# A sixteen-row head load ahead of a streaming attention kernel, with two moved steps in its start

## The chip, the core and the metric

The kernel runs on 1 core of one Trainium2 chip. The metric is the device time of one execution in microseconds (us); lower is better. Before and after are compared on the same chip.

## The reference

One decoding step of attention with grouped queries: 32 query heads of 128 numbers, 8 heads of keys and values, 65536 positions each, all in bf16. Four query heads share one key head.

```python
B, Hq, Hkv, Sq, Sk, D = 1, 32, 8, 1, 65536, 128
def reference(q, k, v):
    rep = Hq // Hkv
    k = jnp.repeat(k, rep, axis=1)
    v = jnp.repeat(v, rep, axis=1)
    scores = jnp.einsum("bhqd,bhkd->bhqk", q, k) * D ** -0.5
    p = _softmax(scores, axis=-1)
    return jnp.einsum("bhqk,bhkd->bhqd", p, v)
```

Keys and values are read once: 8 x 65536 x 128 x 2 bytes, twice, which is 268.4 MB.

## The kernel before, in words

**Tiles.** A unit is 16384 positions of one key head: 128 partitions, on each of which lie T = 128 positions of D = 128 numbers, so 32 KB for each partition. There are 4 units for each key head. Two units make a pair; the 16 pairs (NP) are the laps. One pair of keys or of values is 128 rows of 64 KB, 8 MB.

**One lap.** TensorE transposes the keys of a unit in groups of 8 tiles (`pe_transposes`, L131) into four PSUM buffers `trb`; VectorE copies three groups out of four (L197) and ScalarE the fourth (L194) into `ktb`; TensorE multiplies them with the four queries of the head in `qcur` (`pe_scores`, L140). VectorE takes the maximum of the scores (L228), GpSimd reduces it over the partitions (L390), ScalarE computes the exponentials into `pts` (L346), and TensorE multiplies with the values (`pe_values`, L158). A running maximum and sum rescale what was there before.

**Buffers and loads.** SyncE issues all loads of keys and values in order, on one queue. `kbuf` takes 64 KB for each partition, a whole pair of keys; in laps 1 to 12 the second half is copied from there to `bbuf`, by GpSimd and ScalarE (L204, L355), so that `kbuf` comes free early. `vbuf` takes a pair of values. In lap 0 the keys come as four loads of 2 MB, 128 rows of 16 KB each (`K_PIECES`, L404): two into `kbuf` and two into `bbuf`. Then follow two value loads of 128 rows of 32 KB (L434). The next key load (L416) waits until TensorE is through with `kbuf` (`kfree`) and the copies are done (`cfree`); the next value load (L437) waits for `vfree`, which VectorE gives after TensorE's last product of the pair (L293, L306). In the last lap the values come in small pieces, so that TensorE can follow.

**The start.** VectorE builds the identity `ident` that the transposes need, and signals it through `t_id` (L323). ScalarE issues the load of the 32 queries, 8 KB (L371), then waits for `t_id` and runs a small exponential (L373), which brings its table load ahead of it, then copies the identity to float32 (L374). TensorE waits for the queries (`q_sem`) and the identity, transposes the queries (L180), and goes into the laps; its first step there is to wait for the first key piece (`kp[0][0]`). GpSimd clears `lw` and runs one all-reduce on it (L381, L382), whose result is not used, and then waits for the first copies. `own` is a helper that lets an instruction signal a semaphore, waits for that, and takes the signal back:

```python
def own(e, ins, s):
    ins.then_inc(s, 1)
    take(e, s)
```

**The end.** When the last values are multiplied, VectorE scales the last four rows (L303), TensorE transposes them (L185), VectorE copies them out (L336), and SyncE stores them (L448). The other rows are stored before.

Of the kernel before, what the change touches and what calls it, by code (L numbers as in the profile page):

```python
# [10 lines left out]
P = 128  # L11
# [10 lines left out]

K_PIECES = ((64, 64), (64, 64))
V_PIECES = ((128,), (44, 56, 20, 8))

# [11 lines left out]
def starts(sizes):  # L39
    return [sum(sizes[:i]) for i in range(len(sizes))]  # L40


def take(e, sem, n=1):

    e.wait_ge(sem, n)
    e.sem_inc(sem, -n)  # L46


def bass_standalone__gqa_softmax__decode_kernel(nc, q, k, v, out):
# [8 lines left out]
    kf, vf, qf, of = k[0], v[0], q[0, :, 0, :], out[0, :, 0, :]  # L58
# [4 lines left out]
    def sb(name, shape, dt):  # L63
        return S(nc.sbuf_tensor(name, shape, dt))

    def sem(name):
        return S(nc.semaphore(name))

    kbuf = sb("kbuf", [P, 2 * T * D], DT.bfloat16)
# [4 lines left out]
    qsb = sb("qsb", [HR, D], DT.bfloat16)  # L74
# [16 lines left out]
    la = sb("la", [P, R], DT.float32)  # L91
    lw = sb("lw", [P, R], DT.float32)
# [12 lines left out]
    kp = [[sem(f"kp{i}_{p}") for p in range(len(K_PIECES[i]))] for i in range(2)]  # L105
    vp = [[sem(f"vp{i}_{p}") for p in range(len(V_PIECES[i]))] for i in range(2)]
    kfree, cfree, bfree = sem("kfree"), sem("cfree"), sem("bfree")
# [2 lines left out]
    trd, tra, evd, eva = sem("trd"), sem("tra"), sem("evd"), sem("eva")  # L110
    qkd, qrdy, pvd = sem("qkd"), sem("qrdy"), sem("pvd")
    cm, cma, ng, exd, sx, lrd, lra = (sem(n) for n in ("cm", "cma", "ng", "exd", "sx", "lrd", "lra"))
    acr, l_sem = sem("acr"), sem("l_sem")
    xd, xa, xg = sem("xd"), sem("xa"), sem("xg")
    q_sem, o_sem, s_x, t_if, t_id, t_o, t_f, t_row = (
        sem(n) for n in ("q_sem", "o_sem", "s_x", "t_if", "t_id", "t_o", "t_f", "t_row"))
# [4 lines that stand above are left out]
# [24 lines left out]
    def pe_values(pe, n, lap):  # L145
        vv = vbuf[:, n * T * D:(n + 1) * T * D].rearrange("p (t d) -> p t d", d=D)
        for t in range(T):
            if n and t == V_PIECES[1][0]:
                with pe.If(lap == NP - 1):
                    take(pe, acr)  # L150
                    pe.matmul(pvb[n][:, 0:R], lhsT=identf[:, :], rhs=acc[:, :], start=False, stop=False)
            if t == 0:
                take(pe, vp[n][0], 16)
                take(pe, exd)
            piece = vp[n][starts(V_PIECES[n]).index(t)] if t and t in starts(V_PIECES[n]) else None
            if piece:
# [7 lines left out]
    def pe_pair(pe, lap):  # L164
        pend = []
        for n in range(2):
            for j in range(G):
                pe_transposes(pe, n, j)
                pend.append((n, j))
                if len(pend) > LAG:  # L170
                    pe_scores(pe, *pend.pop(0))
        while pend:
            pe_scores(pe, *pend.pop(0))
        for n in range(2):
            pe_values(pe, n, lap)

    def tensor_engine(pe):
        pe.wait_ge(q_sem, 16)
        pe.wait_ge(t_id, 1)
        pe.transpose(qps[:, 0:HR], qsb[:, :], ident[0:HR, 0:HR]).then_inc(s_x, 1)  # L180
        pe.wait_ge(t_if, 1)
        with pe.Fori(0, NP) as lap:
            pe_pair(pe, lap)
        pe.wait_ge(t_f, H)
        pe.transpose(trb[0][0:R, 0:P], oT[:, HR - R:HR], ident[:, :]).then_inc(s_x, 1)  # L185
# [13 lines left out]
    def copy_unit(e, lap, second, copies, op, done, x):  # L199

        def copies_now():
            for c in copies:
                off = T * D + c * CB * D
                ins = op(bbuf[:, c * CB * D:(c + 1) * CB * D], kbuf[:, off:off + CB * D])  # L204
                if c != copies[-1]:
                    ins.then_inc(done, 1)
            own(e, ins, x)
            e.sem_inc(done, 1)

        lo, hi = ((w - second + 1) // 2 for w in WHOLE)  # L210
        with e.If(lap < hi):
            if lo:
                with e.If(lap >= lo):
                    copies_now()
                with e.Else():
                    e.sem_inc(done, len(copies))
            else:
                copies_now()
        with e.Else():
            e.sem_inc(done, len(copies))  # L220
# [131 lines left out]
    def act_pair(e, second, lap):  # L352

        def copy(o, i):
            return e.activation(o, i, AF.Copy)  # L355

        for j in (3, 7, 11, 15):
            evict(e, 0, j)
            if j in ACT_COPIES:
                copy_unit(e, lap, second, ACT_COPIES[j], copy, cpa, xa)  # L360
                if j == max(ACT_COPIES):
                    e.sem_inc(cfree, 1)
        for j in (3, 7):
            evict(e, 1, j)
        exps(e, 0, not second)
        for j in (11, 15):
            evict(e, 1, j)
        exps(e, 1, False)

    def scalar_engine(e):  # L370
        e.dma_start(qsb[:, :], qf).then_inc(q_sem, 16)  # L371
        e.wait_ge(t_id, 1)
        e.activation(dscr[:, 0:1], ident[:, 0:1], AF.Exp, scale=1.0)  # L373
        e.activation(identf[:, :], ident[:, :], AF.Copy).then_inc(t_if, 1)  # L374
        with e.Fori(0, H) as lap:
            act_pair(e, False, lap)
            act_pair(e, True, lap)


    def gpsimd_engine(e):  # L380
        own(e, e.memset(lw[:, :], 0.0), xg)  # L381
        own(e, e.partition_all_reduce(la[:, :], lw[:, :], P, bass.bass_isa.ReduceOp.add), xg)  # L382
        with e.Fori(0, H) as lap:
            for u in range(HU):
                if u % 2 == 0:
                    take(e, pgo)
                    copy_unit(e, lap, u // 2, POOL_COPIES, e.tensor_copy, cpg, xg)
                    e.sem_inc(cfree, 1)
                take(e, cm)
                e.partition_all_reduce(cmaxa[:, :], cmax[:, :], P, bass.bass_isa.ReduceOp.max).then_inc(cma, 1)  # L390
            take(e, lrd)
            e.partition_all_reduce(la[:, :], lp[:, :], P, bass.bass_isa.ReduceOp.add).then_inc(lra, 1)  # L392


    def sync_engine(e):
        W = T * D

        def src(x, p):
            h, c = p // 2, p % 2
            return x[h, c * 2 * P * T:(c + 1) * 2 * P * T, :].rearrange("(p t) d -> p (t d)", p=P)  # L400

        def pieces(to, s, sizes, sems):
            for a, w, sm in zip(starts(sizes), sizes, sems):
                e.dma_start(to[:, a * D:(a + w) * D], s[:, a * D:(a + w) * D]).then_inc(sm, 16)  # L404

        def tokens(sems):
            for sm in sems:
                e.sem_inc(sm, 16)

        for p in range(NP):  # L410
            ks, vs = src(kf, p), src(vf, p)
            if p:
                e.wait_ge(kfree, p)
                e.wait_ge(cfree, 2 * p)
            if WHOLE[0] <= p < WHOLE[1]:
                e.dma_start(kbuf[:, :], ks).then_inc(kp[0][0], 16)  # L416
                tokens(kp[0][1:])
            else:
                for n in range(2):
                    if n and p:  # L420
                        e.wait_ge(bfree, p)
                    to, s = bbuf if n else kbuf, ks[:, n * W:(n + 1) * W]
                    if p in (0, NP - 1):
                        pieces(to, s, K_PIECES[n], kp[n])
                    else:
                        e.dma_start(to[:, 0:W], s).then_inc(kp[n][0], 16)
                        tokens(kp[n][1:])
            if p:
                e.wait_ge(vfree, p)
            if WHOLE[0] <= p < WHOLE[1]:  # L430
                tokens(kp[1])
            if p in (0, NP - 2):
                for n in range(2):
                    e.dma_start(vbuf[:, n * W:(n + 1) * W], vs[:, n * W:(n + 1) * W]).then_inc(vp[n][0], 16)  # L434
                tokens(vp[1][1:])
            elif p < NP - 1:
                e.dma_start(vbuf[:, :], vs).then_inc(vp[0][0], 16)  # L437
                tokens(vp[1])
            else:
                for n in range(2):  # L440
                    pieces(vbuf[:, n * W:(n + 1) * W], vs[:, n * W:(n + 1) * W], V_PIECES[n], vp[n])
        e.wait_ge(t_o, H)
        for b, rows in enumerate(OUT_ROWS):
            for r, n in zip(starts(rows), rows):
                e.dma_start(of[r:r + n, b * Q:(b + 1) * Q],
                            orow[b * Q + r:b * Q + r + n, :]).then_inc(o_sem, 16)
        e.wait_ge(t_row, 1)
        e.dma_start(of[HR - R:HR, :], lrow[:, :]).then_inc(l_sem, 16)  # L448

    with nc.Block() as block:  # L450
        block.tensor(tensor_engine)
        block.vector(vector_engine)
        block.scalar(scalar_engine)
        block.gpsimd(gpsimd_engine)
        block.sync(sync_engine)
# [30 lines left out]
```

## Time and profile before

| | |
|---|---|
| time, median of 3 runs | 629.42 us (629.23 to 629.5) |
| time of the profiled execution | 629.39 us |
| its span, first to last instruction | 627.7 us |
| TensorE, VectorE, ScalarE, GpSimd busy | 78%, 50%, 36%, 24% of the span |
| queue q1 (SyncE's loads and stores) | 268.45 MB, 99.2% of 16 DMA engines |
| mean granted TensorE clock | 0.779 |

How to read it: a line such as L404 is a line of the kernel above. A row of the timeline gives the start and the length in us, the engine, the line, the operation, the output and the input tile. SPq, ACTq and so on are the sequencers of the engines; a load's row on them is its issue alone. In a table of stages, a row gives the stage, its length, the busy time and number of instructions of TensorE (matmuls, then weight loads), VectorE, ScalarE and GpSimd, and then the granted clock, the busy share of the 16 DMA engines and their rate in GB/s. Shares can be a little over 1.00 in short stages.

### The profile page before, as it was taken

The page shows a single profiled execution, that of the slowest core. Times are in us where ns is not written, and L with a number is a line of the kernel's source. Part 1 is how long each engine was busy: PE and PEld are TensorE (multiplying, and loading weights), DVE is VectorE, ACT ScalarE, POOL GpSimd, SP SyncE. Part 2 cuts the span into 40 slices and gives each one's busy share as a digit, 9 for nine tenths or more (in the row PEclk, how much of TensorE's full clock was granted, in tenths as well). Part 3 has the DMA queues.
Part 4 walks back from the last instruction along what each step waited for, and adds up shares of the span by engine and source line. Part 5 has one row for each costly group of instructions (what it writes and reads, how often), then busy time and mean ns, then how long its engine had stood idle before and what let it go on. Part 6 is the DMA issues. An engine that isn't in the chain of part 4 may idle for free. (4 is left out here: it accounts for less than half of the span.)

```text
span 627.7 us, 28345 instructions
## 1 busy us (share of the span) xinstructions
PE 490.6 (78%) x12292; PEld 482.2 (77%) x12292; DVE 315.4 (50%) x698; ACT 227.4 (36%) x435; POOL 148.8 (24%) x118
## 2 busy tenths in 40 slices
PE   4673995949959598695986949779596899789896
PEld 4663995949959598695976949779596899789796
DVE  4540653717537174371744617356183565638282
ACT  2230542515425154341534406244062442414141
POOL 0000703307042070520605115060250700000000
PEclk9865876968869598695987959678596787859596
DMA  8999999999999999999999999999999999999997
GB/s 366 433 455 424 434 430 439 422 447 418 451 418 451 409 455 413 455 413 452 413 455 413 455 413 451 418 451 413 443 426 439 430 418 451 418 432 434 417 437 301
DMA packets 6914, 268.59 MB, mean 428 GB/s; under 512 B 1016, under 2 KB 1016, under 8 KB 1272
## 3 DMA queue, kind: packets, MB, share of 16 engines
q1 hardware_dynamic: 6856, 268.45, 99.2%
q8 instruction: 6, 0.10, 0.1%
q14 instruction: 4, 0.03, 0.0%
q10 hardware_dynamic: 48, 0.01, 0.0%
HBM read 268.44 MB, written 0.01 MB: 428 GB/s over the span
## 5 line engine op out<-in xcount | busy, mean ns | idle before, releaser
L197 DVE COPY ktb<-trb 128x1024 bf16<-128x1024 bf16 x384 | 254.5, 690 | 171.6 <-DVEq L46 170.4
L194 ACT ACTIVATE ktb<-trb 128x1024 bf16<-128x1024 bf16 x128 | 131.0, 1023 | 346.3 <-ACTq L46 346.3
L131 PE MATMUL trb<-ident,kbuf 128*128 128x128 bf16 x2048 | 177.6, 245 | 86.9 <-PEq L46 86.9
L131 PEld LDWEIGHTS trb<-ident,kbuf 128*128 128x128 bf16 x2048 | 144.1, 111 | 87.8 <-issue 87.8
L140 PE MATMUL qkb<-qcur,ktb 128*128 128x4 bf16 x4096 | 176.7, 165 | 15.1 <-PEq L46 10.7
L140 PEld LDWEIGHTS qkb<-qcur,ktb 128*128 128x128 bf16 x4096 | 157.4, 97 | 23.2 <-issue 21.5
L204 POOL COPY bbuf<-kbuf 128x2048 bf16<-128x2048 bf16 x72 | 132.8, 1893 | 153.3 <-POOLq L46 153.3
L131 PE MATMUL trb<-ident,bbuf 128*128 128x128 bf16 x2048 | 159.4, 221 | 3.9 <-issue 3.9
L158 PE MATMUL pvb<-pts,vbuf 128*128 128x4 bf16 x4096 | 112.9, 166 | 23.9 <-PEq L46 14.3
L158 PEld LDWEIGHTS pvb<-pts,vbuf 128*128 128x128 bf16 x4096 | 111.0, 102 | 25.4 <-issue 23.3
L131 PEld LDWEIGHTS trb<-ident,bbuf 128*128 128x128 bf16 x2048 | 119.3, 98 | 1.5 <-issue 1.5
L390 POOL PARTITION_ALL_REDUCE cmaxa<-cmax x32 | 11.9, 370 | 281.6 <-POOLq L46 281.6
L346 ACT ACTIVATE pts<-qkb,negm 128x128 bf16<-128x128 f32 x128 | 50.6, 545 | 0.0
L355 ACT ACTIVATE bbuf<-kbuf 128x2048 bf16<-128x2048 bf16 x24 | 45.7, 1902 | 0.0
L346 ACT ACTIVATION_READ_ACCUMULATOR pts<-qkb,negm 128x1 f32 x128 | 35.4, 277 | 0.0
L228 DVE TENSOR_REDUCE cmax<-qkb 128x4 f32<-128x512 f32 x32 | 21.9, 686 | 17.8 <-DVEq L46 17.8
L256 DVE TENSOR_TENSOR acc<-acc,pvb 128x4 f32<-128x4 f32 x16 | 2.5, 158 | 37.7 <-PE pvb L158 37.7
L342 ACT ACTIVATE alpha<-dm 128x4 f32<-128x4 f32 x24 | 4.9, 203 | 43.4 <-ACTq L46 43.4
L392 POOL PARTITION_ALL_REDUCE la<-lp x8 | 3.4, 429 | 36.9 <-POOLq L46 36.9
L238 DVE TENSOR_TENSOR m<-m,cmaxa 128x4 f32<-128x4 f32 x24 | 3.9, 163 | 11.7 <-DVEq L46 11.5
L247 DVE TENSOR_TENSOR acc<-acc,alpha 128x4 f32<-128x4 f32 x24 | 3.9, 162 | 11.6 <-DVEq L46 11.6
L254 DVE COPY acc<-pvb 128x4 f32<-128x4 f32 x8 | 1.3, 162 | 15.5 <-PE pvb L158 15.5
(41 smaller groups left out, 39.0 us busy)
## 6 DMA issues: line engine op xcount, KB each, us to landing
vbuf<-in_v_dram SPq DMA_DIRECT2D x5, 4096.0 KB, 31.1
kbuf<-in_k_dram SPq DMA_DIRECT2D x4, 2048.0 KB, 16.9
bbuf<-in_k_dram SPq DMA_DIRECT2D x4, 2048.0 KB, 21.7
kbuf<-in_k_dram SPq DMA_DIRECT2D x2, 4096.0 KB, 20.1
bbuf<-in_k_dram SPq DMA_DIRECT2D x2, 4096.0 KB, 19.8
vbuf<-in_v_dram SPq DMA_DIRECT2D x1, 1792.0 KB, 32.2
vbuf<-in_v_dram SPq DMA_DIRECT2D x1, 1408.0 KB, 28.4
vbuf<-in_v_dram SPq DMA_DIRECT2D x1, 640.0 KB, 33.3
```

Source lines behind the costliest of these rows:

```text
L131: ins = pe.transpose(trb[j % NTB][:, i * P:(i + 1) * P], kv[:, t, :], ident[:, :])
L140: ins = pe.matmul(qkb[n][:, t * R:(t + 1) * R], lhsT=ktb[:, off:off + P], rhs=qcur[:, :], start=True, stop=True)
L158: ins = pe.matmul(pvb[n][:, 0:R], lhsT=vv[:, t, :], rhs=pts[n][:, t * R:(t + 1) * R], start=t == 0, stop=t == T - 1)
L194: e.activation(dst, trb[j % NTB][:, :], AF.Copy).then_inc(eva, 1)
L197: e.tensor_copy(dst, trb[j % NTB][:, :]).then_inc(evd, 1)
L204: ins = op(bbuf[:, c * CB * D:(c + 1) * CB * D], kbuf[:, off:off + CB * D])
L228: e.tensor_reduce(cmax[:, :], qkb[n][:, :].rearrange("p (t g) -> p g t", g=R), AX.X, ALU.max).then_inc(cm, 1)
L238: own(e, e.tensor_tensor(mn[:, :], mo[:, :], cmaxa[:, :], ALU.max), xd)
L342: e.activation(alpha[:, :], dm[:, :], AF.Exp, scale=scale)
L346: ins = e.activation(pv[:, g, :], sv[:, g, :], AF.Exp, bias=negm[:, g:g + 1], scale=scale, accum_out=rsum[:, g:g + 1])
L355: return e.activation(o, i, AF.Copy)
L390: e.partition_all_reduce(cmaxa[:, :], cmax[:, :], P, bass.bass_isa.ReduceOp.max).then_inc(cma, 1)
```

## The change

Three edits, all ahead of the first lap or in its first loads.

1. SyncE issues a new first load: rows 0 to 15 of the first unit, 32 KB for each, 512 KB in all, with a semaphore of its own (`h_sem`). The two loads that followed for `kbuf`, 128 rows of 16 KB each, become 112 rows of 16 KB each. TensorE waits for `h_sem` ahead of the laps. The bytes are the same, in one load more.
2. ScalarE issues the load of the queries after the small exponential, and so after its table load and after the wait for the identity.
3. GpSimd waits for its memset on a semaphore of its own and does not take the signal back; the wait behind its all-reduce is gone.

```diff
+HEAD = 16
 ...
         pe.wait_ge(t_if, 1)
+        pe.wait_ge(h_sem, 16)
         with pe.Fori(0, NP) as lap:
 ...
     def scalar_engine(e):
-        e.dma_start(qsb[:, :], qf).then_inc(q_sem, 16)
         e.wait_ge(t_id, 1)
         e.activation(dscr[:, 0:1], ident[:, 0:1], AF.Exp, scale=1.0)
+        e.dma_start(qsb[:, :], qf).then_inc(q_sem, 16)
         e.activation(identf[:, :], ident[:, :], AF.Copy).then_inc(t_if, 1)
 ...
     def gpsimd_engine(e):
-        own(e, e.memset(lw[:, :], 0.0), xg)
-        own(e, e.partition_all_reduce(la[:, :], lw[:, :], P, bass.bass_isa.ReduceOp.add), xg)
+        e.memset(lw[:, :], 0.0).then_inc(lws, 1)
+        e.wait_ge(lws, 1)
+        e.partition_all_reduce(la[:, :], lw[:, :], P, bass.bass_isa.ReduceOp.add)
 ...
+            if p == 0:
+                e.dma_start(kbuf[0:HEAD, 0:W], ks[0:HEAD, 0:W]).then_inc(h_sem, 16)
 ...
                     if p in (0, NP - 1):
-                        pieces(to, s, K_PIECES[n], kp[n])
+                        r = 0 if n or p else HEAD
+                        pieces(to[r:P], s[r:P], K_PIECES[n], kp[n])
```

More of the change, by code (lines that the diff above doesn't have):

```diff
@@ L112, in bass_standalone__gqa_softmax__decode_kernel @@
     cm, cma, ng, exd, sx, lrd, lra = (sem(n) for n in ("cm", "cma", "ng", "exd", "sx", "lrd", "lra"))
-    acr, l_sem = sem("acr"), sem("l_sem")
+    acr, l_sem, lws = sem("acr"), sem("l_sem"), sem("lws")
+    h_sem = sem("h_sem")
     xd, xa, xg = sem("xd"), sem("xa"), sem("xg")
```

## The prediction

> **What bounds the kernel now.** I read the page's slices and DMA queues first, then the chain that ended last, then stages of the span, then the timeline of the first microseconds.
>
> ```profile
> span 627.7 us, 28345 instructions
> ...
> DMA  8999999999999999999999999999999999999997
> ...
> q1 hardware_dynamic: 6856, 268.45, 99.2%
> q8 instruction: 6, 0.10, 0.1%
> q14 instruction: 4, 0.03, 0.0%
> ...
> HBM read 268.44 MB, written 0.01 MB: 428 GB/s over the span
> ```
>
> The reader is to see that SyncE's queue q1 keeps the 16 DMA engines occupied for 99.2% of the span, from the second slice to the last but one.
>
> ```profile
> 590.81 32.20 DMA vbuf<-in_v_dram
> 623.01 0.05 issue
> 623.06 2.64 PE pvb L158 x84
> 625.70 0.02 issue
> 625.72 0.17 DVE oT L303
> ```
>
> The chain says the same of the end: the last V load lands at 623.01, TensorE multiplies 84 tiles in 2.64 us, and a short tail follows. Now the stages, with the last two columns the DMA share and the rate:
>
> ```profile
> 0.00:1.50 1.50, 0.00 (x0) 0.00 (x0) 0.39 (x7) 0.33 (x1) 0.62 (x6) 1.00 0.00 0
> 1.50:2.00 0.50, 0.00 (x0) 0.00 (x0) 0.30 (x2) 0.50 (x1) 0.10 (x1) 1.00 1.21 262
> 2.00:2.50 0.50, 0.00 (x0) 0.00 (x0) 0.26 (x2) 0.45 (x1) 0.00 (x0) 1.00 0.59 164
> 2.50:3.00 0.50, 0.00 (x0) 0.00 (x0) 0.47 (x3) 0.00 (x0) 0.00 (x0) 1.00 0.32 132
> 3.00:5.00 2.00, 0.00 (x0) 0.00 (x0) 0.28 (x3) 0.40 (x2) 0.00 (x0) 1.00 0.96 405
> ...
> 20.00:580.00 560.00, 439.70 (x11035) 432.37 (x11034) 283.41 (x615) 208.85 (x394) 146.56 (x108) 0.77 1.00 433
> ```
>
> From 20 to 580 us the loads run at 433 GB/s with a DMA share of 1.00. At that rate the 268.44 MB take 268.44 / 0.433 = 620 us, so all but some 8 us of the span is this one stream. Whatever delays the stream at its head delays the end by as much, since nothing later runs faster than 433 GB/s; whatever delays compute by less than the stream's lead costs nothing. The execution behind these rows took 629.39 us, 1.69 us more than its span, and the median of the runs is 629.42, so a sum made against 629.39 holds for the median too.
>
> **The change part by part.** Here is the start, and the two later loads that show the lead:
>
> ```profile
> 0.72 0.42 ACTq L371 DMA_DIRECT2D qsb<-in_q_dram  x1
> 0.72 0.89 SPq L404 DMA_DIRECT2D kbuf<-in_k_dram  x2
> 1.17 0.43 POOL L382 PARTITION_ALL_REDUCE la<-lw  x1 [0.35 <-POOLq L46]
> 1.17 1.28 ACT L373 ACT_TABLE_LOAD   x1 [1.17 <-PEq L471]
> 3.26 0.20 ACT L373 ACTIVATE dscr<-ident 128x1 f32<-128x1 bf16 x1 [0.81 <-DVE ident L323]
> 5.33 0.20 PE L180 MATMUL pvb<-ident,qsb 32*128 32x32 bf16 x1 [5.33 <-DMA qsb<-in_q_dram]
> 8.47 3.57 PE L131 MATMUL trb<-ident,kbuf 128*128 128x128 bf16 x32 [2.94 <-PEq L46]
> ...
> 22.58 0.33 SPq L416 DMA_DIRECT2D kbuf<-in_k_dram  x1
> 26.85 0.37 POOL L390 PARTITION_ALL_REDUCE cmaxa<-cmax  x1 [25.25 <-POOLq L46]
> 58.01 0.33 SPq L437 DMA_DIRECT2D vbuf<-in_v_dram  x1
> ...
> 626.49 0.25 SPq L448 DMA_DIRECT2D out_dram<-lrow  x1
> ```
>
> And for the loads issued in the first 25 us, the time from issue to landing (median):
>
> ```profile
> vbuf<-in_v_dram SPq DMA_DIRECT2D x2, 4096.0 KB, 35.8
> kbuf<-in_k_dram SPq DMA_DIRECT2D x2, 2048.0 KB, 9.8
> bbuf<-in_k_dram SPq DMA_DIRECT2D x2, 2048.0 KB, 19.3
> qsb<-in_q_dram ACTq DMA_DIRECT2D x1, 8.0 KB, 4.6
> kbuf<-in_k_dram SPq DMA_DIRECT2D x1, 40.6
> ```
>
> **GpSimd's shorter program.** A wait and two semaphore decrements go; the memset and the all-reduce stay, with the wait between them. GpSimd ends this work at 1.60 (1.17 + 0.43) and starts its next at 26.85. The 25.25 us of idling hide either sign; without that cover the edit would be worth the 0.35 us ahead of the all-reduce at the most. Cost 0.
>
> **The queries' load behind the table load.** ScalarE issued it at 0.72 and its table load started at 1.17. Now the table load can start about 0.45 us sooner, but the load goes behind the small activation that waits for the identity (3.26, ending 3.46). Issued at some 3.4 us and with the same 4.6 us, it lands at 8.0 instead of 5.33. Behind it on ScalarE is only the copy of the identity, 0.42 us later. TensorE's first wait is for these queries, so all its transposes queue behind it, and VectorE and ScalarE's evictions behind those. But TensorE started the K transposes only at 8.47, when K landed, and 8.0 plus the 0.20 us transpose of the queries is still before it. Cost 0, with 0.27 us to spare against the old start. If the cover goes, there is a second one: the V load issued at 58.01 is the first that waits for TensorE closely, while the K load in front of it is still in flight until 63.2 (22.58 + 40.6). The time from the first issue to the first bytes was about 0.8 to 1.3 us (0.72 to between 1.50 and 2.00), so the lead is some 4 us (63.2 - 58.01 - 1.1). TensorE may start 4 us later, relative to the stream, before a DMA engine runs dry.
>
> **SyncE issues one DMA more.** The first two K issues took 0.89 us, 0.45 each; a store of 4 rows took 0.25. The new first issue of 16 rows lies between 0.25 and 0.45. Everything behind it on SyncE, the rest of K and V, is issued that much later, but each DMA engine has one row of 32 KB meanwhile: 512 KB over all, 1.21 us at 433 GB/s. Hidden; uncovered it would be 0.45.
>
> **The first bytes.** In the three half-microseconds from 1.50 to 3.00 the stream moved 0.5 x (262 + 164 + 132) = 279 KB, where 433 GB/s would be 650 KB. The ramp thus costs 0.86 us. A first load with an eighth of the rows, and no queries' load issued beside it, can shorten its issue by 0.20 and at best take the ramp away: a gain between 0 and 1.06 us. Nothing in the trace says how much of the ramp is the writing out of 128 rows and how much is latency that stays; I take the middle, -0.5.
>
> **Sixteen rows into sixteen partitions.** This term decides. All loads of the trace write 128 partitions; a load of 512 KB into 16 partitions that lie side by side is not there. If 433 GB/s is a property of the 16 DMA engines, the head takes 1.21 us, as these bytes would anyway: cost 0. If it is a property of the places written, one partition takes 433 / 128 = 3.38 GB/s, 16 take 54, and the head lasts 9.69 us: cost 8.5. A gain is excluded here, because the 433 GB/s already fill the engines. No row is nearer to one end than the other: the 32 KB row for each engine is like V's first loads, the destination is like none. I take the middle, +4.2, and keep both ends. The stream cannot make it up, since each engine has the same bytes after it as before.
>
> [...]
>
> **112 rows instead of 128, twice.** 7 rows of 16 KB for each engine instead of 8, 3.67 MB in all, 8.5 us at 433 GB/s. By engines the cost is 0; by partitions 112 x 3.38 = 379 GB/s and 9.7 us, cost 1.2. Having taken partitions as counting, I take +1.2 here. If the engines' shares no longer lie apart as in a load of 128 rows, it is more; the range has 4 us for it in place of 1.2.
>
> **The wait for the head, and the first piece.** TensorE waits for the head and the first piece: 512 + 1792 KB instead of 2048, 256 KB or 0.6 us later than the stream's own shift. Against the lead of 4 us: cost 0. The last loads and the output are untouched, and their shift is the stream's.
>
> Sum: 0 + 0 + 0 - 0.5 + 4.2 + 1.2 + 0 = +4.9, and 629.4 + 4.9 = 634.3 us.
>
> **The rivals.**
>
> **No crowding.** The DMA engines set the rate wherever they write, and only the ramp gets shorter: 629.4 - 1.06 to 629.4, so 628.4 to 629.4. For it: a DMA share of 1.00 at 433 GB/s is what 16 busy engines look like. Against it: the same row is what 128 busy partitions look like. 0.23, and it counts as no change.
>
> **Faster.** The ramp goes wholly (-1.06) and GpSimd's shorter program needs one load of code less. Code comes by the same DMA engines: q14's 4 loads have under 0.05% of 16 x 627.7 us, so at most 1.3 us each. If the one that goes was on the engine that ends last, the end comes 2.3 us sooner: 627.1. It decides from 1.26 us on. For it: the chain ends on a load, so the last engine counts. Against it: four loads on sixteen engines, and no row ties one to GpSimd. 0.08.
>
> **The crowding goes on.** The middle case has the head at 524 KB / 5.4 us = 97 GB/s. If the 112 rows are dealt out so that the engines write neighbouring partitions at each moment, their 3.67 MB run at that rate too, 37.8 us instead of 8.5: 629.4 - 0.5 + 4.2 + 29.3 = 662. Against it: loads of 128 rows run at full rate, so the dealing out avoids this there. 0.06.
>
> **The queries come late.** They are now issued behind 16 MB that SyncE has in its queue. If they went behind all of it they would land at some 40 us, and TensorE would use up the lead of 4 us and 27 more: 656. It decides from 12.5 us on (8.47 + 4). Against it: before, they were issued together with the first K loads, whose landing took 9.8 us, and landed in 4.6, so they pass large loads. 0.03.
>
> **How the numbers follow.** Forecast 0.60, no crowding 0.23, faster 0.08, crowding that goes on 0.06, late queries 0.03. The forecast's own range is 629.4 - 1.06 + 0 + 0 = 628.4 at the bottom, shared with the second case, to 629.4 + 8.5 + 1.2 - 0.5 = 638.6 at the top; 4 us instead of 1.2 for the 112 rows with the middle of the head stays inside (637.1). The range 628.4 to 638.6 leaves out the faster case and the two far ones, 0.17. About 0.2%, 1.26 us, is what a measurement of this kernel can tell from no change. Of the forecast's 0.60 I put 0.03 under 1.26 us, since its head can lie near its lower end. Slower: 0.57 + 0.06 + 0.03 = 0.66. Within: 0.23 + 0.03 = 0.26. Faster: 0.08.
>
> **What would show it.** In the profile after, the rate in the first 10 us decides: right if the windows up to about 6 us stay well under 433 GB/s, near 100, and if the first K transpose comes at 13 to 15 us; wrong if they reach 405 by 3 us and the transpose comes at about 9. The middle stage should be 433 GB/s as before, with the last V landing near 628. The first bytes should come before 1.7 us. GpSimd's row at 26.85 and the issue at 58.01 should move by the stream's shift and no more. The queries' transpose should come near 8 us, and the first wait on TensorE that ends last should be K's or the head's. A rate of the middle stage other than 433, or a DMA share under 1.00 near 60 us, would prove the sum wrong at its base.

## The result and the profile after

The changed kernel takes 637.32 us (median; 636.79 to 637.78) where the kernel before, beside it, takes 629.44 (629.23 to 629.5): slower by 7.9 us, a ratio of 1.0125 with a 95% interval of 1.0113 to 1.0138. The page of the changed kernel:

```profile
span 635.4 us, 28345 instructions
...
q1 hardware_dynamic: 6856, 268.45, 99.2%
q8 instruction: 6, 0.10, 0.1%
q14 instruction: 4, 0.03, 0.0%
```

The span is 7.7 us longer, with the same packets and bytes, the DMA engines as occupied as before, and the same number of code loads: a DMA share of 99.2% said nothing of how fast the bytes went. The chain that ended last has only been moved, with its pieces as long as before:

```profile
598.61 32.21 DMA vbuf<-in_v_dram
630.82 0.05 issue
630.87 2.61 PE pvb L161 x84
```

Where the time went is seen in the stages (last two columns: DMA share, GB/s). First two stages of the kernel before that the prediction did not show, then the changed kernel's:

```profile
1.50:1.80 0.30, 0.00 (x0) 0.00 (x0) 0.15 (x2) 0.30 (x1) 0.10 (x1) 1.00 0.95 218
...
8.00:20.00 12.00, 11.11 (x213) 11.07 (x214) 7.72 (x12) 3.07 (x3) 0.00 (x0) 1.00 1.01 433
```

```profile
1.50:1.80 0.30, 0.00 (x0) 0.00 (x0) 0.15 (x2) 0.30 (x1) 0.00 (x0) 1.00 2.86 437
...
5.00:8.00 3.00, 0.00 (x0) 0.00 (x0) 0.00 (x0) 0.00 (x0) 0.00 (x0) 1.00 0.76 158
8.00:20.00 12.00, 5.53 (x80) 5.45 (x81) 3.55 (x9) 1.02 (x1) 0.00 (x0) 1.00 1.01 282
20.00:580.00 560.00, 436.99 (x11006) 429.76 (x11004) 282.12 (x608) 207.15 (x385) 146.73 (x108) 0.78 1.00 433
```

A packet's bytes, and its time with them, are put down at its start, so the short stages at the beginning read as counts: 218 GB/s for 0.3 us is four packets of 16 KB, 437 is four packets of 32 KB. As many packets had started by 1.80 us as before; the head did not start the stream sooner. From 8 to 20 us it ran at 282 GB/s instead of 433, with a DMA share of 1.01: the engines were occupied with packets that took longer. From 20 to 580 us the rate is 433 GB/s as before. Nearly the whole loss lies in the first 20 us.

The first steps, and the loads issued in the first 25 us (median time to landing), of the changed kernel:

```profile
0.72 0.39 SPq L421 DMA_DIRECT2D kbuf<-in_k_dram  x1
1.17 0.87 SPq L409 DMA_DIRECT2D kbuf<-in_k_dram  x2
3.26 0.39 ACTq L377 DMA_DIRECT2D qsb<-in_q_dram  x1
13.45 0.20 PE L183 MATMUL pvb<-ident,qsb 32*128 32x32 bf16 x1 [13.45 <-DMA qsb<-in_q_dram]
14.68 3.57 PE L134 MATMUL trb<-ident,kbuf 128*128 128x128 bf16 x32 [1.03 <-PEq L48]
```

```profile
kbuf<-in_k_dram SPq DMA_DIRECT2D x2, 1792.0 KB, 16.5
kbuf<-in_k_dram SPq DMA_DIRECT2D x1, 512.0 KB, 6.9
qsb<-in_q_dram ACTq DMA_DIRECT2D x1, 8.0 KB, 10.1
```

The reader is to see the head, a quarter of a 2 MB load, taking 6.9 us to land, and the queries 10.1 instead of 4.6. TensorE still waited for K after them: its first K transpose comes at 14.68.

### The profile page after: what moved, and what is told of

It is laid out like the page before. It is cut to its first block, busy times and chain, and to the rows that moved or that the text cites. A ratio compares the mean times of both kernels' runs of the same rounds, so it can differ in the third digit from the quotient of the medians.

```text
span 635.4 us, 28345 instructions
## 1 busy us (share of the span) xinstructions
PE 488.1 (77%) x12292; PEld 479.8 (76%) x12292; DVE 315.3 (50%) x698; ACT 227.7 (36%) x435; POOL 149.0 (23%) x118
## 3 DMA queue, kind: packets, MB, share of 16 engines
q1 hardware_dynamic: 6856, 268.45, 99.2%
## 5 line engine op out<-in xcount | busy, mean ns | idle before, releaser
L242 DVE TENSOR_TENSOR m<-m,cmaxa 128x4 f32<-128x4 f32 x24 | 3.9, 163 | 11.7 <-DVEq L48 11.5
```

What stands on the lines that cost most here:

```text
L242: own(e, e.tensor_tensor(mn[:, :], mo[:, :], cmaxa[:, :], ALU.max), xd)
```

## The experiments

Theory A: what slows the change is where it writes, 16 partitions side by side and then uneven shares of 112. Rivals, as they come up: the late queries, the read side, a fixed price for short or early loads, the form of a 112-row load.

**Without the head.** The head's load, its wait and the 112 rows are undone; the other two edits stay.

```diff
-        pe.wait_ge(h_sem, 16)
 ...
-            if p == 0:
-                e.dma_start(kbuf[0:HEAD, 0:W], ks[0:HEAD, 0:W]).then_inc(h_sem, 16)
 ...
-                        r = 0 if n or p else HEAD
-                        pieces(to[r:P], s[r:P], K_PIECES[n], kp[n])
+                        pieces(to, s, K_PIECES[n], kp[n])
```

> The head is undone, the other two edits stay (shorter GpSimd program, queries' load behind the table load). Theory A (the partitions written are what makes the change slow): all of the 7.9 us goes, 629.4 within 0.5 us, and the K loads in the first 10 us run at 400 GB/s and more again. Rival: the late queries, which landed 10.1 us after their issue with the change, hold TensorE and cost part of it: then 631 or more. The queries should land about 4.6 us after their issue, as before, since no crowded load is in front of them.

Measured: 628.96 us beside 629.25 for the kernel before, ratio 0.9995 (0.9986 to 1.0005). All of the loss goes. The other two edits together can't be told from no change. The queries landed later than expected all the same, 6.4 us after their issue, and TensorE's first K transpose came at 10.04 instead of 8.47; the lead of the stream covered that.

**The head alone.** The queries' load and GpSimd's program are as before.

```diff
+        e.dma_start(qsb[:, :], qf).then_inc(q_sem, 16)
         e.wait_ge(t_id, 1)
         e.activation(dscr[:, 0:1], ident[:, 0:1], AF.Exp, scale=1.0)
-        e.dma_start(qsb[:, :], qf).then_inc(q_sem, 16)
 ...
+        own(e, e.memset(lw[:, :], 0.0), xg)
+        own(e, e.partition_all_reduce(la[:, :], lw[:, :], P, bass.bass_isa.ReduceOp.add), xg)
```

> The head alone, the queries' load and GpSimd's program as before. Theory A: 637.3 within 0.7 us, the same as the whole change. Rival (the queries' late landing counts): the queries are issued at 0.72 again, and the time falls by 1 us or more, to 636 or less.

Measured: 637.6 us (637.36 to 637.78), ratio 1.0133 (1.0116 to 1.015). The whole loss, with the queries early. Two rows of its timeline show why they don't matter:

```profile
8.11 0.20 PE L183 MATMUL pvb<-ident,qsb 32*128 32x32 bf16 x1 [8.11 <-DMA qsb<-in_q_dram]
14.85 2.40 PE L134 MATMUL trb<-ident,kbuf 128*128 128x128 bf16 x21 [6.53 <-PEq L48]
```

The queries come 5.3 us sooner than with the whole change, and K's first transpose is at 14.85, no sooner.

**Sixteen neighbouring rows, eight times.** In the kernel before, the first K load is cut by rows.

```diff
+        pe.wait_ge(h_sem, 128)
 ...
+                    if p == 0 and n == 0:
+                        c = K_PIECES[0][0] * D
+                        for r in range(8):
+                            e.dma_start(kbuf[16 * r:16 * r + 16, 0:c], ks[16 * r:16 * r + 16, 0:c]).then_inc(h_sem, 16)
+                        tokens(kp[0][:1])
+                        e.dma_start(kbuf[:, c:W], ks[:, c:W]).then_inc(kp[0][1], 16)
```

> The kernel before with its first K load, 128 rows of 16 KB, cut into eight loads of 16 rows each, rows 0-15, 16-31 and so on; all else as before. The bytes are the same, 2 MB. Theory A (16 neighbouring partitions are written at some 105 to 113 GB/s, as the head's 512 KB in about 4.7 us say): 2.1 MB take 18.6 to 20 us instead of 4.85, so +14 us, 643. Rival B (reading 16 neighbouring rows of DRAM is slow): the same 643. Rival C (each load of few rows costs a fixed part, 3.5 us for the head): eight times 3.5 us, 657; or, if the head was slow only because it was the first load, 629.4 to 633.

Measured: 640.9 us, ratio 1.0185 (1.0164 to 1.0205), +11.7 us. Not 14: the rate is 122 GB/s in the stage of these loads (below); my 105 to 113 had the head's start-up in it. Neither a fixed price for each load (657) nor one for the first load (633) fits.

**Sixteen rows, eight apart.** The same, with both sides strided.

```diff
-                            e.dma_start(kbuf[16 * r:16 * r + 16, 0:c], ks[16 * r:16 * r + 16, 0:c]).then_inc(h_sem, 16)
+                            e.dma_start(kbuf[r:P:8, 0:c], ks[r:P:8, 0:c]).then_inc(h_sem, 16)
```

> As the run with eight loads of 16 neighbouring rows, but load r takes the rows r, r+8, r+16 and so on, in DRAM and in SBUF alike. [...] If only neighbourhood counts: 629.4. [...] Rival C: the same time as with neighbouring rows, 643 or more.

Measured: 634.14 us, ratio 1.0077 (1.0057 to 1.0097), +4.9. As many loads, as many rows, as many bytes, and 6.8 us less. These rows run at half of the 433 GB/s of 128 rows, 218 (below); if neighbourhood alone counted, it would have been 629.4 us.

**Which side it is: writes in a block, reads strided; and the other way round.**

```diff
+                            e.dma_start(kbuf[16 * r:16 * r + 16, 0:c], ks[r:P:8, 0:c]).then_inc(h_sem, 16)
```

> Eight loads of 16 rows for the first K piece again, but each writes 16 neighbouring partitions (16r to 16r+15) and reads the DRAM rows r, r+8, r+16 and so on. It puts other keys into the partitions of one piece in the first lap, so the keys of that piece meet other positions' values; amount and kind of the work are the same. Theory A (the written partitions set the rate): as with neighbouring rows on both sides, 640.9 within 1 us. Rival B (neighbouring DRAM rows set it): as with strided rows on both sides, 634.1 within 1 us.

```diff
+                            e.dma_start(kbuf[r:P:8, 0:c], ks[16 * r:16 * r + 16, 0:c]).then_inc(h_sem, 16)
```

> The counterpart: each of the eight loads reads 16 neighbouring DRAM rows and writes the partitions r, r+8, r+16 and so on; keys of that piece are again in other partitions than their positions' values. Theory A: 634.1 within 1 us. Rival B: 640.9 within 1 us.

Measured: 640.66 and 634.12 us, ratios 1.0181 (1.0161 to 1.0202) and 1.0077 (1.0057 to 1.0098). The time goes with the written partitions and not with the rows read. The stage of these loads says it in the rate; in order, 16 neighbouring rows on both sides, then only written so, from 4 to 16 us:

```profile
4.00:16.00 12.00, 0.20 (x1) 0.10 (x1) 0.59 (x4) 0.00 (x0) 0.00 (x0) 1.00 0.98 122
```

```profile
4.00:16.00 12.00, 0.20 (x1) 0.10 (x1) 0.59 (x4) 0.00 (x0) 0.00 (x0) 1.00 1.00 123
```

and strided on both sides, then only written so, from 4 to 11 us:

```profile
4.00:11.00 7.00, 0.00 (x0) 0.00 (x0) 0.33 (x3) 0.00 (x0) 0.00 (x0) 1.00 1.04 218
```

```profile
4.00:11.00 7.00, 0.00 (x0) 0.00 (x0) 0.33 (x3) 0.00 (x0) 0.00 (x0) 1.00 1.03 218
```

122 and 123 against 218 and 218, at a DMA share of about 1 in all four: rival B, the read side, falls.

**The 112 rows written out.** The changed kernel's first load of 112 rows becomes seven loads of 16 rows. If each engine takes seven neighbouring rows of the 112 in turn, these loads are the same traffic written out, and time and rate stay as they are.

```diff
+        pe.wait_ge(h_sem, 16 * 8)
 ...
+                            for r in range(7):
+                                e.dma_start(kbuf[HEAD + r:P:7, 0:c], ks[HEAD + r:P:7, 0:c]).then_inc(h_sem, 16)
+                            tokens(kp[0][:1])
+                            e.dma_start(kbuf[HEAD:P, c:W], ks[HEAD:P, c:W]).then_inc(kp[0][1], 16)
```

> The changed kernel, with its first load of 112 rows of 16 KB replaced by seven loads of 16 rows, load r taking the rows 16+r, 23+r, 30+r and so on, 7 apart; head and second 112-row load stay. [...] Rival D (a load of 112 rows is dealt to fewer engines, or is slow as a form): loads of 16 rows use all engines, so the first piece runs at another rate and the time falls by 1.5 us or more; if the 112 rows were dealt row by row over the engines, the second piece would be as slow as loads of 16 neighbouring rows, some 125 GB/s, which the changed kernel's 255 to 315 GB/s from 8 to 20 us already speak against.

Measured: 636.52 us, ratio 1.0115 (1.0095 to 1.0136), 0.8 us under the whole change; the two intervals overlap. From 5 to 12 us, the changed kernel first, then this one:

```profile
5.00:12.00 7.00, 0.00 (x0) 0.00 (x0) 0.00 (x0) 0.00 (x0) 0.00 (x0) 1.00 0.90 233
```

```profile
5.00:12.00 7.00, 0.20 (x1) 0.10 (x1) 0.59 (x4) 0.00 (x0) 0.00 (x0) 1.00 0.92 233
```

The same rate (the head, which lands at 7.6 us, is still in this stage), so a load of 112 rows behaves as if each engine took seven neighbouring rows in turn. That the rows are in fact dealt so is inferred from this likeness; the profile does not name the engine of a packet. Rival D falls: with a DMA share of 1.01, the mean of the 16 engines, from 8 to 20 us no engine is left out. Seven loads are no slower than one here, so cutting a load up is not what cost 4.9 us in the strided run. By the same reading that run gives each engine eight neighbouring rows in turn, at 218 GB/s; a whole load of 128 rows runs at 433, so it must then be dealt in another way, and no run shows in which.

**A head of 64 rows.**

```diff
-HEAD = 16
+HEAD = 64
```

> One size changed: the head has 64 rows of 32 KB (2 MB) instead of 16, the two loads behind it 64 rows of 16 KB instead of 112. [...] Rival C (few rows for each engine are slow, one row the slowest): 4 rows for each engine crowd less than 1, so under +4 us, 633 or less. Rival E (each partition takes 3.4 GB/s at most): 64 rows at 217 GB/s, +9.6 us, 639; the 16 rows of the head, at over 100 GB/s instead of 54, already speak against it.

Measured: 639.34 us, ratio 1.016 (1.0143 to 1.0177), +10.1. By that the 4.2 MB of the head and the two loads behind it took 10.1 us over the 9.7 that they take at 433 GB/s, which is 212 GB/s: half rate again, with 64 rows on 16 engines, four for each. More rows for each engine don't help if half of the partitions are left out (rival C falls), and a loss comes without any load of 112 rows. Rival E, 3.4 GB/s for each partition, fits this run too; it falls with the 16 neighbouring rows at 122 GB/s, which are 7.6 GB/s each.

**The same 512 KB, 128 rows wide.**

```diff
-HEAD = 16
+HEAD = 16 * 128
 ...
-                e.dma_start(kbuf[0:HEAD, 0:W], ks[0:HEAD, 0:W]).then_inc(h_sem, 16)
+                e.dma_start(kbuf[:, 0:HEAD], ks[:, 0:HEAD]).then_inc(h_sem, 16)
 ...
+                            e.dma_start(kbuf[:, HEAD:c], ks[:, HEAD:c]).then_inc(kp[0][0], 16)
+                            e.dma_start(kbuf[:, c:W], ks[:, c:W]).then_inc(kp[0][1], 16)
```

> The changed kernel with a head of the same 512 KB in another shape: 128 rows of 4 KB instead of 16 rows of 32 KB; the two loads behind it have 128 rows again (12 KB and 16 KB). The other two edits stay. Theory A: all partitions are written at once, so nothing is crowded, and the time is that of the run without a head, 629.0 within 0.4 us. Rival F (a small load more at the head costs something in itself, by its landing or by its wait on TensorE): 630 or more. If an early first piece helps at all, it would be under 628.7; the stream bounds the end, so theory A does not expect it.

Measured: 629.29 us beside 629.32, ratio 1.0 (0.9991 to 1.0009). An early small load costs nothing in itself, and brings nothing: the stream bounds the end. Its head lands in 4.0 us after its issue:

```profile
kbuf<-in_k_dram SPq DMA_DIRECT2D x1, 512.0 KB, 4.0
```

This and the run without a head are the best kernels of the study, and neither can be told from the kernel before.

**Half of the uneven bytes.** The head has 16 rows of 16 KB, the first K load 112 rows, the second 128.

```diff
+                e.dma_start(kbuf[0:HEAD, 0:c], ks[0:HEAD, 0:c]).then_inc(h_sem, 16)
 ...
+                            e.dma_start(kbuf[HEAD:P, 0:c], ks[HEAD:P, 0:c]).then_inc(kp[0][0], 16)
+                            e.dma_start(kbuf[:, c:W], ks[:, c:W]).then_inc(kp[0][1], 16)
```

> The changed kernel with half of the uneven bytes: a head of 16 rows of 16 KB, one load of 112 rows of 16 KB, and the second K load with 128 rows again. Theory A: the loss goes with the bytes that are written unevenly, so half of 8.3 us (the changed kernel against the run without a head), 633.2 within 1 us. Rival G (a fixed price for the head at the start of the stream, most of the loss): 635.5 or more. Rival H (the loss comes mainly from engines that got out of step and stay so): also over 635.

Measured: 632.14 us, ratio 1.0049 (1.0033 to 1.0064): 3.2 us over the run without a head, and 1.1 under the expected 633.2, just outside its 1 us. A fixed price for the head (rival G) and engines that stay out of step as the main loss (rival H) both fall, but the loss isn't quite in proportion: the second half of the uneven bytes costs some 5 us where the first costs 3.

**112 rows ahead of the head.**

```diff
-                e.dma_start(kbuf[0:HEAD, 0:W], ks[0:HEAD, 0:W]).then_inc(h_sem, 16)
 ...
+                            e.dma_start(kbuf[HEAD:P, 0:c], ks[HEAD:P, 0:c]).then_inc(kp[0][0], 16)
+                            e.dma_start(kbuf[0:HEAD, 0:W], ks[0:HEAD, 0:W]).then_inc(h_sem, 16)
+                            e.dma_start(kbuf[HEAD:P, c:W], ks[HEAD:P, c:W]).then_inc(kp[0][1], 16)
```

> The changed kernel with the order of the first three loads changed: 112 rows of 16 KB, then the head of 16 rows of 32 KB, then 112 rows of 16 KB. It asks what a load of 112 rows costs with no crowded head in front of it. Theory A (neighbouring shares of seven rows clash by themselves): the first 1.8 MB run well under 433 GB/s, at 250 to 330, from the first bytes on, and the time stays at 636 to 638. Rival H (the 112-row loads are slow only because the head leaves the engines out of step): the first load of 112 rows runs at over 400 GB/s, lands within 7.5 us of its issue, and the time is under 635.5.

Measured: 636.44 us, ratio 1.0117 (1.01 to 1.0134). From 3 to 7 us, with nothing crowded in front, this kernel and then the kernel before:

```profile
3.00:7.00 4.00, 0.00 (x0) 0.00 (x0) 0.28 (x3) 0.51 (x2) 0.00 (x0) 1.00 1.03 319
```

```profile
3.00:7.00 4.00, 0.20 (x1) 0.10 (x1) 0.88 (x7) 0.40 (x2) 0.00 (x0) 1.00 1.00 424
```

A load of 112 rows is slow by itself, 319 against 424 GB/s. Behind the head the second one ran at 295 from 15 to 20 us, so some of the rest may be engines out of step; that share was not measured.

## Why the prediction was right

The sign, the mechanism and the place were right: the stream is the bound, the first 20 us are slower by what is written, and the end is moved by that. The size was short, 4.9 us against 7.9, with the measured time inside the range. That it lies inside is in part luck: the head's term was too high, the 112 rows' too low by more, and the top of the range rested on 8.5 us for the head. Of the signs that were named, K's first transpose came at 14.68, within 13 to 15; the queries' came at 13.45 and not near 8. Step by step:

- **Base.** 433 GB/s from 20 to 580 us before and after; a delay of the stream is a delay of the end. Right.
- **GpSimd's program, and the rival of a code load less.** Cost 0 is borne out (no head: 0.9995). Queue q14 has 4 loads before and after, so no code load went.
- **The queries' load.** Cost 0 was right, the landing wrong: I kept the 4.6 us of an idle start, and behind loads in flight they took 6.4 us without the head, and 10.1 with it. The cover moved too, since K came at 14.68. The head-alone run shows that nothing hung on it.
- **One issue more on SyncE.** 0.39 us, within 0.25 to 0.45, hidden. But 128 rows had taken 0.45 with their gap, so the shorter load saved next to nothing in issue.
- **The first bytes, -0.5.** Not there. Four packets had started by 1.80 us in either kernel, with 16 rows in the first load as with 128. The wide head gave nothing either.
- **Sixteen rows, +4.2.** The right term, too large: the same 512 KB land in 6.9 us as 16 rows and in 4.0 as 128 rows, so 2.9 (by the time of the packets 2.0, below). The middle between engine and partition as the limit was a guess; the limit is neither. At 122 GB/s, 16 neighbouring partitions take 7.6 GB/s each, more than the 3.38 of that bound. Measured were 122 to 123 GB/s for 16 neighbouring partitions, 218 for 16 that lie eight apart, 212 for the loads of 64 rows, and 433 for 128; what in the chip sets these rates, no run shows.
- **112 rows, +1.2.** This is the term that failed in size. I took the bound by partitions, 379 GB/s; it ran at 282 from 8 to 20 us, so by that rate the 3.67 MB take 13.0 us instead of 8.5, a cost of 4.5 (by the time of the packets 5.4, below). The case was named in the step, shares that no longer lie apart, with 4 us kept for it in the range, and should have been the value: once a load's partitions count, it matters which are written together, 122 GB/s for 16 neighbouring ones and 218 for 16 that lie eight apart. The run with the 112 rows first shows that they are slow by themselves, 319 GB/s where 128 rows ran at 424. One row of the head and seven of the 112 for each engine were the author's estimate, 16 and 112 rows over 16 engines.
- **The new sum.** 2.9 + 4.5 = 7.4 of the measured 7.9. The time of the packets divides it otherwise. The DMA share times the length of a stage is the time that the packets started in it take, for each of the 16 engines; first the kernel before, then the changed one, each with the first 512 KB and the next 3.67 MB:

```profile
1.50:3.60 2.10, 0.00 (x0) 0.00 (x0) 1.31 (x8) 1.29 (x3) 0.10 (x1) 1.00 0.79 252
3.60:12.20 8.60, 3.94 (x43) 3.86 (x44) 2.67 (x7) 0.09 (x2) 0.00 (x0) 1.00 1.00 427
```

```profile
1.50:3.00 1.50, 0.00 (x0) 0.00 (x0) 1.03 (x6) 0.50 (x1) 0.00 (x0) 1.00 2.46 350
3.00:19.10 16.10, 4.63 (x59) 4.55 (x60) 2.95 (x10) 1.24 (x3) 0.00 (x0) 1.00 0.87 228
```

The head took 2.46 x 1.50 = 3.7 us of each engine, where its bytes took 0.79 x 2.10 = 1.7 before: 2.0 more. The 112 rows took 0.87 x 16.10 = 14.0 us instead of 8.6: 5.4 more. So most of the loss is the 112 rows, and the head is its smaller part. Some 0.5 is left of the 7.9. Part of it lies right behind, where the loads of 128 rows ran below their rate for a while, 413 GB/s from 20 to 25 us; that engines out of step cause this was not shown.
- **The wait for the head, and the lead.** Cost 0. The next loads were issued at 28.44 and 61.10, and the rate stayed 433 GB/s from 20 to 580 us, at a DMA share of 1.00, so no engine ran dry. I had expected the second of them, and GpSimd's row at 26.85, to move by the stream's shift. GpSimd's moved by 6.0, to 32.82, and the issue by 3.1 only, from 58.01; TensorE's last products of that lap moved as little, from 55.95 to 59.02, and where the lap made up the rest was not measured.
- **The rivals.** No crowding, and a crowding that stays at the head's rate through the 112 rows, are both refuted by the 282 GB/s. Late queries are refuted by the head-alone run.

## What to carry to other kernels

When loads bound a kernel, keep every load as wide as the full set of partitions, also the small first one (here 433 GB/s to 128 partitions, 122 to 16 neighbouring ones): an occupied DMA engine is not a fast one (a DMA share of 1.01 at 282 GB/s), and time lost at the head of a bound stream is lost at the end (nearly all of the 7.9 us). To get a first piece early, cut along the row (128 rows of 4 KB landed in 4.0 us) and not across rows (6.9 us for 16 rows), though here neither brought a gain. To tell a write limit from a read limit, change the order on one side at a time: two runs beside the two with both sides alike settled it here, by the rate in a stage and not by the total alone.

## What was not expected of the hardware

Eight loads of 16 rows to every eighth partition ran at 218 GB/s, to 16 neighbouring partitions at 122, with the same bytes and the same DMA share of about 1. A load of 112 rows ran at 319 GB/s by itself and at about 280 behind the head, where 128 rows run at 433: an eighth of the rows taken away costs a quarter to a third of the rate. The issue of a load took 0.39 us for 16 rows and 0.40 for 128 (the wide head), and in the kernel before and the changed one alike the first four packets had started by 1.80 us. The rows alone don't set the issue: eight loads with strided writes took 5.03 us to issue, eight with neighbouring ones 3.62.
